# Linear attention and a Fourier feed-forward on one core: the channel transform on twice folded rows, some steps on POOL, and new ranks for the first part

## The chip, the cores and the metric

The kernel runs on one NeuronCore of a Trainium2 chip. Its engines work side by side and are joined by semaphores: TensorE (PE in the profile, with its weight loads as PEld), VectorE (DVE), ScalarE (ACT), GpSimd (POOL) and SyncE (SP, which here only issues DMA transfers). The metric is the device time of one execution in microseconds (us). Several executions are timed, and their median counts.

## The reference

```python
kv  = einsum('bhsd,bhse->bhde', k, v)            # 8 batches, 8 heads, 576 tokens, 64 per head
out = einsum('bhsd,bhde->bhse', q, kv)
x   = out / sqrt(mean(out*out, -1) + 1e-6) * g_norm   # then heads side by side: [8, 576, 512]
X     = fft(fft(x, axis=1), axis=2)              # over the tokens, then over the channels
u     = x + real(X)
un    = (u - mean(u)) / sqrt(var(u) + 1e-6)
y     = u + maximum(un @ w_ch1, 0) @ w_ch2       # 512 -> 2048 -> 512
```

The weights of the feed-forward arrive as 64-bit floats, which the kernel takes apart in 32-bit words.

## The kernel before, in words

**First part: attention and transform, by batch.** For each of the eight batches `plan_kv` (L527) multiplies keys and values (bank `ps_k`, L574), `plan_q` (L631) turns the queries (`ps_q`, L643), and `plan_out` (L657) multiplies them with the result (`ps_o`, L669). Tokens lie in three tiles t of 96 or 97 rows; a row holds token p and its mirror S − p side by side, which is the fold over the tokens. `plan_y` and `plan_fold` (L716, L752) scale the rows by their root mean square and fold them over the channels: channel d plus channel 512 − d, 256 columns per side (L785 on VectorE), then sum and difference of the two sides on POOL (L792). ACT and POOL split the result into a high part `xh` and a low part `xl` for fp32r matmuls (L798, L801). Everywhere a product of two split operands takes three matmuls, `passes`: high·high, high·low, low·high.

**The two transforms.** `plan_seq` (L807) multiplies the folded rows with the token matrix `cs` (290 columns), once for each of two parts (cosine, sine) and two channel halves ch of 128; ACT and VectorE split the product (`ps_f`, L816) into the pair `pt` (L830, L834). `plan_chn` (L840) multiplies `pt` with the channel matrix `cd` (258 columns) for each tile and part: two halves times three passes, summed in one bank (L851). ACT copies the cosine part out (L863), VectorE adds the sine part with either sign (L871), and the sums are added to x (L883, L886: on VectorE for batch 0, else on POOL). `plan_turn` (L917) then transposes x into `unT` (`ps_t`, L942; split at L951, L954), blocks of 512 tokens.

**Weights and feed-forward.** `plan_w` (L964) loads a pair of weights as 64-bit words and makes 32-bit floats of them: absolute value on ACT (`w_clear`, L352), then five VectorE steps (`w_steps`: a clamp L359, shifts and masks L360 to L366, a product L369), a sum, and a split. Three pairs (NA = 3) are made early, in the first part; four more at its end; the others in the second part. With the early ones `plan_early` (L1021) runs the first three of the 16 hidden slices for all nine token blocks inside the first part: `ffn1` (`ps_h`, L424) and `ffn2` (`acc`, L442). The second part runs the remaining slices.

**What sets the order.** The first part is a list of operations with an engine, a cost in ns, a rank, predecessors and buffers. `Plan.run` (L155) is a list scheduler: on each engine, the ready operation of the lowest rank whose buffers are free goes next. `rank(b, stage)` is 10 b + stage, with the stages KV, QT, OUT, SCL, FOLD, SEQ, CHN, NRM as 0 to 7, less 40 for batch 0; the early feed-forward has 1000 and more. `SHIFT` (L58) adds to the ranks of single stages on single engines, keyed by stage, engine and rounded rank. `W_CONV` and `W_RANK` (L42) are the ranks of the early weights' work and loads. The order is pinned up to 95 us of the plan's time; behind that the compiler orders by itself. `plan_spare` (L486) puts in 45 operations of two 512-column matmuls each, whose result nobody reads (`ps_s`, L494), wherever TensorE would wait. Buffers come from rings of fixed sizes (`RINGS`, L72), among them eight PSUM banks (`p8`).

## Time and profile before

| what | before |
|---|---|
| median of 3 runs | 1024.85 us (1022.36 to 1027.26) |
| the profiled execution | 1022.79 us |
| its span, first to last instruction | 1021.0 us |
| busy: PE / PEld | 1002.3 / 844.0 us |
| busy: DVE / ACT / POOL | 475.3 / 324.8 / 314.4 us |
| granted TensorE clock | 1.00 |
| moved by DMA | 140.74 MB, 137 GB/s over the span |

The span is cut into stretches and each engine's busy time is given for them; the groups collect instructions by line and shape, with the mean duration of one. The chain of waits follows the work that ended last back to its start. Matmuls are pipelined, so the duration of one (390 ns for 512 columns) is longer than the distance to the next; the chain's pieces, divided by their count, give that distance. The transforms end at 319 us; the early feed-forward goes on after them.

### The profile page before, as it was taken

What the parts mean: (1) busy time and instruction counts of PE and PEld (TensorE: products, weight loads), DVE (VectorE), ACT (ScalarE), POOL (GpSimd) and SP (SyncE); (2) the same over time, 40 slices, a digit from 0 to 9 for tenths busy, and PEclk for the clock granted to TensorE, in tenths of its full rate; (3) what the DMA queues carried; (4) which work ended last, traced back from release to release, by engine and by line L of the source; (5) the groups of instructions that cost most, each with busy time, mean ns of one, the idle gap of its engine ahead of it and who ended that gap; (6) DMA issues with size and microseconds to landing.
All of it is one profiled execution on the core that took longest, in us unless ns stands there. A gap on an engine that the chain in (4) does not pass through costs nothing.

```text
span 1021.0 us, 15425 instructions
## 1 busy us (share of the span) xinstructions
PE 1002.3 (98%) x6070; PEld 844.0 (83%) x6070; DVE 475.3 (47%) x847; ACT 324.8 (32%) x657; POOL 314.4 (31%) x328
## 2 busy tenths in 40 slices
PE   5999999999999999999999999999999999999997
PEld 5898888889888888888888888888888888888886
DVE  4897656654788879997131313131221311311211
ACT  2666556554644434344221202121121120210110
POOL 0526768775675132235722303020020010100000
PEclk9999999999999999999999999999999999999999
DMA  9989778664346775645553514230320400400101
GB/s 250 212 230 282 181 209 258 162 170 131 137 163 213 268 253 191 236 129 170 161 179 86 180 59 150 82 125 0 141 67 1 165 21 1 165 0 1 42 1 42
DMA packets 109260, 140.74 MB, mean 138 GB/s; under 512 B 51854, under 2 KB 76482, under 8 KB 104580
## 3 DMA queue, kind: packets, MB, share of 16 engines
q1 hardware_dynamic: 105652, 132.28, 41.9%
q0 software_dynamic: 1920, 6.29, 1.9%
q10 hardware_dynamic: 1616, 1.18, 0.5%
q8 instruction: 48, 0.79, 0.3%
q14 instruction: 24, 0.20, 0.1%
HBM read 88.33 MB, written 51.40 MB: 137 GB/s over the span
## 4 chain that ended last, share of the span: by engine, by line
PE 97%; DMA 1%; ACT 0%; POOL 0%; DVE 0%; issue 0%; SPq 0%; DVEq 0%; POOLq 0%
PE ps_h L424 38%; PE acc L442 38%; PE ps_o L669 4%; PE ps_f L816 4%; PE ps_f L851 4%; PE ps_k L574 3%; PE ps_s L494 2%; PE ps_q L643 2%; PE ps_t L942 2%; DMA qt<-in_q_dram 1%; PE ps_w L383 1%; DMA vm<-in_v_dram 0%; POOL x L883 0%; ACT x L686 0%; DVE uu L1324 0%
## 5 line engine op out<-in xcount | busy, mean ns | idle before, releaser
L424 PE MATMUL ps_h<-unTh,w 128*128 128x512 f32 x1152 | 356.6, 391 | 1.2 <-ACT fq L647 1.2
L442 PE MATMUL acc<-w,hh 128*128 128x512 f32 x1152 | 345.5, 390 | 0.0
L437 DVE SCALAR_TENSOR_TENSOR hl<-ps_h,hh 128x512 fp32r<-128x512 f32 x144 | 99.1, 688 | 371.8 <-ACT hh L434 367.5
L442 PEld LDWEIGHTS acc<-w,hh 128*128 128x128 f32 x1152 | 215.1, 188 | 44.3
L424 PEld LDWEIGHTS ps_h<-unTh,w 128*128 128x128 f32 x1152 | 214.8, 188 | 44.8 <-ACT fq L647 1.4
L434 ACT ACTIVATE hh<-ps_h 128x512 fp32r<-128x512 f32 x144 | 85.8, 596 | 454.0 <-PE ps_h L424 439.2
L424 PE MATMUL ps_h<-unTl,w 128*128 128x512 f32 x576 | 224.3, 389 | 0.0
L442 PE MATMUL acc<-w,hl 128*128 128x512 f32 x576 | 213.5, 389 | 0.0
L424 PEld LDWEIGHTS ps_h<-unTl,w 128*128 128x128 f32 x576 | 108.1, 188 | 22.6
L442 PEld LDWEIGHTS acc<-w,hl 128*128 128x128 f32 x576 | 108.1, 188 | 22.6
L1271 POOL DMA_INDIRECT uu<-u_scr,rowidx x24 | 23.2, 968 | 285.1 <-DVE uu L1324 177.9
L709 POOL TENSOR_TENSOR x<-x,gb 96x512 f32<-96x512 f32 (+1 forms) x42 | 55.0, 1330 | 45.7 <-ACT x L686 40.3
L1290 POOL TENSOR_TENSOR uu<-uu,up 128x512 f32<-128x512 f32 x36 | 45.7, 1298 | 45.2 <-ACT up L1287 45.2
L1234 POOL TENSOR_TENSOR w<-wap,w 128x512 fp32r<-128x512 f32 x18 | 26.4, 1467 | 75.3 <-ACT w L1233 69.1
L669 PEld LDWEIGHTS ps_o<-kvt,fq 64*96 64x96 f32 (+1 forms) x864 | 40.9, 162 | 5.7 <-issue 4.0
L1324 DVE SCALAR_TENSOR_TENSOR uu<-acc,rs_yb,uu 128x512 f32<-128x512 f32 x36 | 25.2, 744 | 42.5 <-PE acc L442 42.5
L669 PE MATMUL ps_o<-kvt,fq 64*96 64x64 f32 (+1 forms) x864 | 44.4, 248 | 0.0
L696 DVE TENSOR_REDUCE ss<-ps_o 96x8 f32<-96x512 f32 (+1 forms) x48 | 32.0, 682 | 26.5 <-ACT ps_o L691 26.3
L792 POOL TENSOR_TENSOR xe<-ab 96x256 f32<-96x256 f32 (+1 forms) x46 | 38.0, 845 | 18.7 <-DVE ab L785 17.9
L816 PE MATMUL ps_f<-cs,xh 96*128 96x290 f32 (+1 forms) x192 | 39.0, 300 | 0.0
L1278 DVE BATCH_NORM_STATS2 bst<-uu 128x6 f32<-128x512 f32 x36 | 24.5, 687 | 29.0 <-DMA uu<-u_scr,rowidx 19.8
L851 PE MATMUL ps_f<-cd,pt 128*96 128x258 f32 (+1 forms) x288 | 37.8, 285 | 0.0
(114 smaller groups left out, 1022.4 us busy)
## 6 DMA issues: line engine op xcount, KB each, us to landing
raw<-in_moe_w_ch_dram SPq DMA_DIRECT2D x32, 512.0 KB
unT_scr<-unTh SPq DMA_DIRECT2D x9, 1024.0 KB
unT_scr<-unTl SPq DMA_DIRECT2D x9, 1024.0 KB
part_scr<-part SPq DMA_DIRECT2D x36, 256.0 KB
unTh<-unT_scr SPq DMA_DIRECT2D x9, 1024.0 KB
unTl<-unT_scr SPq DMA_DIRECT2D x9, 1024.0 KB
up<-part_scr SPq DMA_DIRECT2D x36, 256.0 KB
out_dram<-uu SPq DMA_DIRECT2D x36, 256.0 KB
```

Of the source, the lines that this page charges most:

```text
L424: nc.tensor.matmul(ps, w[c][:, kc * P : (kc + 1) * P], unT[a][:, kc, :], start=(idx == 0), stop=(idx == 3 * KC - 1),)
L434: nc.scalar.activation(hh, ps, AF.Relu)
L437: nc.vector.scalar_tensor_tensor(hl, ps, 0.0, hh.bitcast(F32), ALU.max, ALU.subtract)
L442: nc.tensor.matmul(acc, hpair[a][:, i * P : (i + 1) * P], w[c], start=(first and n == 0), stop=(last and n == 2),)
L574: nc.tensor.matmul(ps.t[s * D : (s + 1) * D, pr * D : (pr + 1) * D], km[:, s, j, :] if j < 4 else kr[:, h, :], vm[:, s, j, :] if j < 4 els ...
L669: nc.tensor.matmul(pss[s].t[:n, at : at + D], fqs[side].t[half, m, :n], kvt.t[half, m], start=True, stop=True,)
L696: nc.vector.tensor_reduce(ss.t[0][:n, :, t, s::2], pss[s].t[:n].rearrange("p (u m e) -> p u m e", u=2, e=D), AX.X, ALU.add,)
L709: nc.gpsimd.tensor_tensor(v_, v_, gb[:n].unsqueeze(1).to_broadcast([n, H, D]), ALU.mult)
L792: nc.gpsimd.tensor_tensor(o[:, s], a[:, 0], a[:, 1], ALU.subtract if s else ALU.add)
L816: nc.tensor.matmul(ps.t[:, :NS], xs[t].t[a][:n, part, ch * P : (ch + 1) * P], cs[:n, part, c, t, :], start=(idx == 0), stop=(idx == 8),)
L851: nc.tensor.matmul(ps.t[:n, :ND], pt.t[a][:, part, ch, offs[t] : offs[t] + n], cd[:, part, c, ch, :], start=(idx == 0), stop=(idx == 5),)
L1290: nc.gpsimd.tensor_tensor(us[j][i], us[j][i], part, ALU.add)
```

## The change

**The channel transform.** Two matmul operations of a part are made first, one per channel half. ACT copies the second out of PSUM (`far`), VectorE writes its sum with the first into one bank and the difference into the other, and each is split as before. For even output columns only one of these is needed, for odd ones the other. So `plan_chn` multiplies each with 130 columns of one parity (`NE`) instead of both halves with 258. For this the first fold lays the upper channel half out in reverse order, in three operations, and the matrix is loaded with its columns sorted by parity (`plan_dft_d`). Channel 128 is its own partner; channel 256, which stands in its place in the other half, goes into the odd columns alone and into the sum of element zero (`x0`): `paired` is 0 in partition 127 and 1 elsewhere, and that row of the odd cosine columns gets 1 added.

```diff
@@ plan_fold
-            nc.scalar.activation(
-                x0[:n, t, b : b + 1], xv(0)[:, 0:1], AF.Identity, bias=xv(1)[:, 0:1]
-            )
+            nc.vector.tensor_reduce(x0[:n, t, b : b + 1], x.t[:n, :: DH], AX.X, ALU.add)
...
-            nc.vector.tensor_tensor(
-                two_of(ab), xx[:, :, 1 : DH + 1], xx[:, ::-1, DM - 1 : DH - 1 : -1], ALU.add
-            )
+            for at, lo, hi, step in ((0, 1, P + 1, 1), (P, DH - 1, P, -1), (DH - 1, DH, DH + 1, 1)):
+                width = (hi - lo) * step
+                nc.vector.tensor_tensor(
+                    two_of(ab)[:, :, at : at + width],
+                    xx[:, :, lo:hi:step],
+                    xx[:, ::-1, DM - lo : DM - hi : -step],
+                    ALU.add,
+                )
@@ plan_seq, for each part, after both matmul operations
+        def out_():
+            nc.scalar.copy(far.t, pss[1].t[:, :NS])
+        def add():
+            p0, p1 = (ps.t[:, :NS] for ps in pss)
+            if part == 0:
+                nc.vector.scalar_tensor_tensor(p1, far.t, paired, p0, ALU.mult, ALU.add)
+            else:
+                nc.vector.tensor_tensor(p1, p0, far.t, ALU.add)
+        def sub():
+            p0 = pss[0].t[:, :NS]
+            if part == 0:
+                nc.vector.scalar_tensor_tensor(p0, p0, paired, far.t, ALU.mult, ALU.subtract)
+            else:
+                nc.vector.tensor_tensor(p0, p0, far.t, ALU.subtract)
+        f = op("ACT", 410, r - D2, out_, mms[1:], [pss[1], far])
+        e = op("DVE", 450, r - D2, add, [mms[0], f], [far] + pss)
+        o = op("DVE", 450, r - D2, sub, [e], [far, pss[0]])
+        for ps, parity, after in ((pss[1], part, e), (pss[0], 1 - part, o)):
...
@@ plan_chn
-                for ch in range(2):
-                    for a, c in passes:
+                for e in range(2):
+                    for idx, (a, c) in enumerate(passes):
                         nc.tensor.matmul(
-                            ps.t[:n, :ND],
-                            pt.t[a][:, part, ch, offs[t] : offs[t] + n],
-                            cd[:, part, c, ch, :],
+                            ps.t[:n, e * NE : (e + 1) * NE],
+                            pt.t[a][:, part, e, offs[t] : offs[t] + n],
+                            cd[:, part, c, e, :],
                             start=(idx == 0),
-                            stop=(idx == 5),
+                            stop=(idx == 2),
                         )
...
-            mms.append(op("PE", 720, r, mm, dones + [dft["d", part]], [ps, pt]))
+            mms.append(op("PE", 500, r, mm, dones + [dft["d", part]], [ps, pt]))
...
+        def both(a):
+            return a[:n, : 2 * NE].rearrange("p (e k) -> p k e", e=2)[:, : ND // 2]
```

The copy of the cosine part and the two sums with the sine part (L863, L871) read the bank through `both`, so that the columns come out in their order.

**Steps on POOL.** The clamp of the three early weight pairs (six tiles) goes from VectorE and PSUM to POOL and SBUF, and the subtraction that gives the token matrix's low part goes from VectorE to POOL. Later weights are clamped on VectorE as before.

```diff
@@ plan_dft, token matrix only
         c = op(
-            "DVE", 200 + 1.6 * size if key == "s" else 200 + size, r,
-            lambda: nc.vector.tensor_tensor(lo, raw.t[:n, :size], hi.bitcast(F32), ALU.subtract),
+            "POOL", 2300, r,
+            lambda: nc.gpsimd.tensor_tensor(lo, raw.t[:n, :size], hi.bitcast(F32), ALU.subtract),
@@ plan_w
+        high = ps if late_ else pf
+        d = op("ACT", 670, r, lambda: w_clear(raw.t, high.t), [a], [raw, ps, pf, src])
+        if late_:
+            d = op("DVE", 690, r, lambda: w_clamp(nc.vector, ps.t), [d], [ps])
+        else:
+            d = op("POOL", 1000, r, lambda: w_clamp(nc.gpsimd, pf.t), [d], [pf])
```

**The order.** The ten shifts of ranks are replaced by 25. Among them: the first pair's weight loads go from rank −60 to −27.5, behind keys and values (−40), the queries of one tile (−38.5) and both matrices (−37, −35); the other queries of batch 0 go from −39 (with a shift of −1.5 before) to 2.5; the VectorE steps of the second weight pair from 5 to 138.5, the ACT steps of the third from 6 to 118.

```diff
 SHIFT = {
-    ("", "POOL", 20): 18,
-    ("chn", "ACT", -34): 54.5,
-    ("dft", "DVE", -35): 83.5,
-    ("fold", "DVE", -36): -33.5,
-    ("out", "DVE", -58): 31,
-    ("out", "ACT", 2): 157,
-    ("q", "PE", -39): 3,
-    ("q", "PE", 21): -30,
-    ("q", "ACT", 31): -19.5,
-    ("q_load", "DMA", -39): -1.5,
+    ("chn", "DVE", -34): 31,
+    ("chn", "POOL", 16): 76.5,
+    ("chn", "ACT", 26): 113.5,
+    ("chn", "POOL", 26): 29.5,
+    ("chn", "ACT", 36): 60.5,
+    ("chn", "POOL", 36): 104,
+    ("out", "PE", -38): -7.5,
+    ("out", "ACT", -8): 36.5,
+    ("out", "DVE", -8): 40,
+    ("out", "PE", 22): 129,
+    ("out", "ACT", 32): 10.5,
+    ("out", "POOL", 42): 91.5,
+    ("q", "ACT", 41): -31.5,
+    ("q", "PE", 41): 76.5,
+    ("q", "POOL", 41): 42.5,
+    ("q_load", "DMA", -39): 41.5,
+    ("turn", "ACT", 17): 54.5,
+    ("turn", "PE", 17): 10,
+    ("turn", "ACT", 27): 87.5,
+    ("turn", "PE", 27): 193.5,
+    ("w", "DMA", -60): 32.5,
+    ("w", "DVE", 5): 133.5,
+    ("w", "ACT", 6): 112,
+    ("y", "DVE", -37): 100,
+    ("y", "POOL", 23): -28,
 }
```

More of the change, by code (lines that the diff above doesn't have):

```diff
@@ L73 @@
     "p8": 8, "part": 2, "unT": 2, "h": 2 * NA, "qt": 2, "fq": 4, "kvt": 2, "kv": 6, "kr": 2,
-    "x": 8, "raw": 2, "e2": 4, "wk": 2, "xhl": 3, "pt": 1, "two": 2,
+    "x": 8, "raw": 2, "e2": 4, "wk": 2, "xhl": 3, "pt": 1, "two": 2, "far": 1,
 }
@@ L460 @@
     cs = cst.tile([TR + 1, 2, 2, 3, NS], F32R, name="cs")
-    cd = cst.tile([P, 2, 2, 2, ND], F32R, name="cd")
+    cd = cst.tile([P, 2, 2, 2, NE], F32R, name="cd")
+    paired = cst.tile([P, 1], F32, name="paired")
+    nc.vector.tensor_scalar(paired, ident[:, P - 1 : P], -1.0, 1.0, ALU.mult, ALU.add)
     x0 = cst.tile([TR + 1, 3, B], F32, name="x0")
@@ L503, in plan_dft @@
     def plan_dft(part, dst, src, n, r, key):
+        if key == "d":
+            plan_dft_d(part, r)
+            return
         size = src.shape[-2] * src.shape[-1]
@@ L793, in even @@
             return go
-        f = op("DVE", 690, r, fold, ms, [x, ab, xe], port=True)
-        z = op("ACT", 300, r, zero, ms + [i_x0], [x])
+        f = op("DVE", 860, r, fold, ms, [x, ab, xe], port=True)
+        z = op("DVE", 80, r, zero, ms + [i_x0], [x])
         e = [op("POOL", 830, r, even(s), [f], [ab, xe]) for s in range(2)]
@@ L1108 @@
         pt = Buf("pt", lambda: [one.tile([P, 2, 2, NS], F32R, name=f"pt{i}") for i in range(2)])
-        pts = [plan_seq(b, grp, xhl, pt, lows) for grp in range(4)]
+        pts = sum((plan_seq(b, part, xhl, pt, lows) for part in range(2)), [])
         for t in range(3):
@@ L1217, in sum_w @@
         w_clear(raw, ps)
-        for step in w_steps(raw, ps, pf):
+        w_clamp(nc.vector, ps)
+        for step in w_steps(raw, ps, pf, ps):
             step()
```

113 lines of the change are left out of this document (72 added, 41 removed).

## The prediction

> **What bounds the kernel now.** I read the head of the page first, then the chain of waits piece by piece, then the groups by shape, then the windows of the first 400 us. Columns of the page's first lines: busy time, share, instructions; then the span in 40 slices.
>
> ```profile
> span 1021.0 us, 15425 instructions
> PE 1002.3 (98%) x6070; PEld 844.0 (83%) x6070; DVE 475.3 (47%) x847; ACT 324.8 (32%) x657; POOL 314.4 (31%) x328
> ...
> PE   5999999999999999999999999999999999999997
> ...
> DVE  4897656654788879997131313131221311311211
> ```
>
> TensorE works through the whole span, so a change is worth what it takes from TensorE's stream plus what it does to TensorE's idle time. A busy TensorE can still be slowed inside a group of matmuls, so I need the pace of each kind. The chain of waits gives it (start, length, what):
>
> ```profile
> 1.77 8.50 DMA qt<-in_q_dram
> ...
> 10.36 0.88 PE ps_q L643 x4
> ...
> 24.18 5.61 PE ps_o L669 x128
> ...
> 37.85 0.88 PE ps_k L574 x20
> ...
> 77.36 5.48 PE ps_h L424 x24
> ...
> 276.90 4.84 PE ps_f L816 x36
> 285.53 4.30 PE ps_f L851 x36
> ...
> 360.44 2.73 PE ps_h L424 x12
> ```
>
> A sequence-transform matmul (290 columns) takes 4.84 / 36 = 134.4 ns, a channel-transform matmul (258) 4.30 / 36 = 119.4, a feed-forward matmul (512) 2.73 / 12 = 227.5. From 258 to 512 columns that is 108.1 / 254 = 0.426 ns a column, and that line gives 133.0 at 290, close to the row: these three kinds are limited by streaming their columns, and the loading of their weights is hidden.
>
> Idle time of TensorE is 1021.0 − 1002.3 = 18.7 us: 10.4 before the first matmul, 5.4 in the last 21 us, and some 3 in gaps. The gaps are this small because something fills them. Below: the first and the last stretch (PE, PEld, DVE, ACT, POOL, granted clock, DMA share, GB/s), and all matmuls of the filler, first and last.
>
> ```profile
> 0.00:25.00 25.00, 14.64 (x150) 12.33 (x152) 10.95 (x20) 6.05 (x11) 0.96 (x9) 1.00 1.06 250
> 1000.00:1021.00 21.00, 15.64 (x70) 12.61 (x68) 4.79 (x7) 1.20 (x2) 0.00 (x0) 0.99 0.13 51
> ```
> ```profile
> L494 PE MATMUL ps_s<-still x90: 387/397/588, 13.4 to 90.4; 128*128 128x512 f32 x90
> ```
>
> The filler (ps_s) does no useful work, is issued a fixed number of times and is spent at 90 us; from 77 us the early feed-forward (ps_h) takes over. Both kernels pay for the filler, 90 × 227.5 ns = 20.5 us.
>
> **The channel transform.** It removes 288 matmuls of 258 columns and puts in 288 of 130: two parities × three passes × two parts × 24 tiles, where there were two channel halves × three × two × 24. Before, that is 288 × 119.4 = 34.4 us of the chain. No fp32r matmul so narrow is in the trace. Streaming alone, by the line above, would be 119.4 − 128 × 0.426 = 64.9 ns. But each matmul also loads 96 or 97 columns of weights, and that sets a floor of its own. Weight loads by shape (the number of columns is the last of the loaded shape; then busy, mean ns):
>
> ```profile
> L851 PEld LDWEIGHTS ps_f<-cd,pt 128*96 128x96 f32 x192 | 23.6, 162 | 0.3
> L816 PEld LDWEIGHTS ps_f<-cs,xh 96*128 96x128 f32 x128 | 20.5, 189 | 0.0
> L1131 PEld LDWEIGHTS ps_o<-cs,x0h 96*8 96x8 f32 x4 | 0.4, 89 | 0.2
> ```
>
> From 96 to 128 columns a load grows by 27 / 32 = 0.84 ns a column, from 8 to 96 by 73 / 88 = 0.83. So 97 columns need 81 ns of loading, whatever is streamed meanwhile. The attention output shows this floor at work: ps_o above are 64 pairs on the two halves of the array's rows, 97 weight columns and only 64 streamed ones each, and a pair takes 5.61 / 64 = 87.7 ns. I take 87.7, the nearest row (the same number of weight columns with a shorter stream): 288 × (119.4 − 87.7) = **9.1 us less**. Ends: 64.9 ns gives 15.7 us less; no gain at 119.4; losses are among the rivals.
>
> The Trainium skill ("TensorE: Matmul & The Clock Gate", Part 3, The mechanism) says that a weight load overlaps matmuls in flight only when the row group differs. By that, narrow matmuls would be a poor exchange, since loading and streaming would stand one behind the other; the 258-column row speaks against it, as 81 ns of loading and 258 × 0.426 = 110 of streaming fit in 119.4. The isolated gap on that page of the Trainium skill (Back-to-back issue gap) would make it 130 / 2.4 + 2.5 = 56.7 ns, an estimate that gives 18.1 us less; it gives 110.0 at 258, where the row has 119.4.
>
> **What the second fold adds.** Rows of the first 320 us, by shape, and one of line L785 over the whole span (shortest/median/longest):
>
> ```profile
> L785 DVE TENSOR_TENSOR ab<-x 96x512 f32<-96x512 f32 x15 | 16.0, 1064 | 3.6 <-POOL x L886 3.4
> L774 DVE TENSOR_TENSOR x<-x,ps_y 96x512 f32<-96x512 f32 x32 | 20.0, 676 | 0.1
> L834 DVE TENSOR_TENSOR pt<-ps_f,pt 128x290 fp32r<-128x290 f32 x32 | 13.8, 454 | 9.4 <-ACT pt L830 9.2
> L359 DVE TENSOR_SCALAR ps_a<-ps_a 128x512 f32<-128x512 f32 x9 | 6.2, 694 | 5.4 <-ACT ps_a L352 5.4
> L520 DVE TENSOR_TENSOR cs<-draw,cs 97x870 fp32r<-97x870 f32 x2 | 2.0, 1022 | 0.0
> L954 DVE TENSOR_TENSOR unTl<-ps_t,unTh 128x4 fp32r<-128x4 f32 x7 | 1.2, 164 | 0.0
> L594 DVE TENSOR_TENSOR kvt<-ps_k,gb 128x256 f32<-128x256 f32 x1 | 0.4, 424 | 3.2 <-PE ps_k L574 3.2
> ```
> ```profile
> L785 DVE TENSOR_TENSOR ab<-x x23: 673/717/1861, 32.5 to 299.5; 96x512 f32<-96x512 f32 x15, 97x512 f32<-97x512 f32 x8
> ```
> ```profile
> L830 ACT ACTIVATE pt<-ps_f 128x290 fp32r<-128x290 f32 x32 | 12.9, 415 | 15.0 <-PE ps_f L816 14.7
> L779 ACT ACTIVATE x<-x 96x1 f32<-96x1 f32 x16 | 4.7, 291 | 3.9 <-DVE x L774 3.8
> ```
>
> Per batch and part ACT gets a copy out of PSUM (415 ns) and VectorE an addition and a subtraction of 290 columns (454 each): over 16 parts ACT 6.6 us, VectorE 14.5. The first fold becomes two operations of half the width and one of two elements: 2 × 424 + 164 = 1012 against 1064 at the mean here, but 0.3 us more where the old one ran undisturbed (median 717), so 0 to 8 us over 24. The sum of element zero goes from ACT (24 × 0.291 = 7.0 us less) to VectorE (24 × 0.164 = 3.9 at most). From VectorE go six clamps (4.2 us) and two subtractions on the token matrix (2.0). Net: VectorE +12 to +20 us, ACT about even. The strided reads of the channel results I cost at nothing: the old fold reads an operand backwards and takes 673 at its shortest, the scaling in plain order 676. Where does the VectorE time lie?
>
> ```profile
> 25.00:100.00 75.00, 75.00 (x901) 64.31 (x898) 61.47 (x105) 45.98 (x100) 33.31 (x46) 1.00 0.94 240
> 100.00:325.00 225.00, 222.01 (x1956) 194.99 (x1955) 146.26 (x271) 124.13 (x290) 156.69 (x168) 1.00 0.61 181
> ```
>
> Columns are PE, PEld, DVE, ACT, POOL. From 100 to 325 us VectorE has 79 us free. From 25 to 100 it is 82% busy, but most of the 6.2 us leaves that stretch, and the new ranks push VectorE's steps on the second pair of weights far back. So I cost it at 0. What hides it is the early feed-forward on TensorE; the price without that cover is the longer way from a sequence product to its channel product: a copy, two VectorE operations and a second split, 0.415 + 2 × 0.454 = 1.3 us a batch, 10.4 us over eight.
>
> **What moves to POOL.** Six clamps and two subtractions of 870 columns:
>
> ```profile
> L709 POOL TENSOR_TENSOR x<-x,gb 96x512 f32<-96x512 f32 x28 | 37.3, 1349 | 24.6 <-ACT x L686 19.2 <-DMA qt<-in_q_dram 5.4
> L731 POOL TENSOR_SCALAR m<-ss 97x48 f32<-97x48 f32 x7 | 1.6, 230 | 0.6
> ```
>
> At 1.35 us per 512 columns that is 6 × 1.35 + 2 × 2.3 = 12.7 us; a clamp costs between 0.23 and 1.35, and I take the latter, which has its width. In 25 to 100 us POOL is busy 33 of 75, so it fits. Each weight's chain grows by 0.65, and folds queued behind on POOL wait up to 1.35 each; TensorE has filler then. Cost 0, at worst 6 × 0.65 + 2 × 1.3 = 6.5 us.
>
> **The order of the first part.** SP's queue now begins with two weight loads:
>
> ```profile
> 0.74 0.99 SPq L349 DMA_DIRECT2D raw<-in_moe_w_ch_dram  x2
> ```
>
> This 1 MB goes behind the keys, the queries of one tile and both matrices; the queries of the other two tiles go behind it. At 250 GB/s (first stretch) 1 MB is 4.2 us, by which keys and values arrive earlier. TensorE starts on them, before 10.36, but a pair of heads (0.88 us of matmul) needs 512 KB, 2.1 us of transfer, so it starts and waits. Against that, the moved queries have 2304 + 480 + 660 + 516 + 1024 KB ahead of them and 960 of their own, 6.1 MB or 24.3 us: just where the first ps_o stood (24.18), so the first tile moves up and the others stay or slip by the landing. I count 2 us less idle time, between 4.2 less and 2 more. The remaining new ranks reorder VectorE, ACT, POOL and TensorE work of batches 1 to 4; I put them at 0, between the 3 us of gaps and the loss of the fourth rival.
>
> **Sum.** The profiled execution took 1022.79 us, its span 1021.0. Of the former: −9.1 − 2.0 = 1011.7. The median of the runs shown, 1024.85, is 2.06 above that execution, so as a median I predict **1013.7 us**, 1.1% faster.
>
> **Rivals**, as medians. (1) Streaming alone limits: 64.9 ns, 15.7 + 2.0 less, 1007.2. For it: loads are hidden in all three fp32r rows. Against: the 87.7 of ps_o. 0.10. (2) The longer way to the channel product is not covered: +10.4, 1024.1, no change. For it: the ps_f buffers are held longer, and there are eight banks; against: the early feed-forward lies between, in all but the first batches. 0.11. (3) Slower: a narrow fp32r matmul runs at the pace of plain fp32.
>
> ```profile
> 48.73 0.93 PE ps_w L383 x8
> ```
>
> The only full products of 128 columns in the trace are these, plain fp32, two records to a product, 0.93 / 4 = 232 ns. At 130 columns that is 236 ns, 288 × (236 − 119.4) = 33.6 us more: 1024.85 − 2.0 + 33.6 = 1056.5. It decides from 119.4 ns. All fp32r rows are of 258 columns or wider, so no row excludes it; all of them lie on one line, so none hints at it. 0.06. (4) The early feed-forward starts late: the second and third pairs of weights now wait behind VectorE and ACT work of all batches, the filler is spent, and TensorE idles for the block it had at 75 to 125 us, 72 × 227.5 ns = 16.4 us: 1030.1, at the edge between the same and slower. For it: ranks of 118 and more for these steps; against: a low rank only yields, and VectorE has gaps. 0.10. (5) Loading and streaming stand one behind the other: 87.7 + 64.9 = 152.6 ns, 9.6 us more, 1032.5; the 258-column row speaks against it. It is the overlap rule of the Trainium skill cited above. 0.03.
>
> **How the numbers follow.** Forecast 0.60. Taking 0.5% (5.1 us, about what a measurement of this kernel can tell) as the bound: faster 0.60 + 0.10 = 0.70; same 0.11 + 0.06 of the fourth = 0.17; slower 0.04 + 0.06 + 0.03 = 0.13. The range takes in rival 1 with the 3 us of gaps (1004) and reaches past rival 2 to 1026; left out are rivals 3 and 5, most of 4, and a little below.
>
> **What would show it.** Right: 36 channel matmuls in 3.0 to 3.2 us of the chain; feed-forward unchanged at 227 ns; a first matmul of keys before 10 us; filler still 90 records; TensorE's busy time near 992 us. Wrong: channel matmuls at 65 or above 119 ns; idle time of TensorE that ends on VectorE's split, on the added copy, or on a weight; the first ps_h well behind 77 us with gaps ahead of it.

## The result, and the profile after

The kernel after the change takes 1029.98 us (median of 11 runs, 1028.74 to 1031.65), the kernel before 1023.94 (11 runs, 1022.28 to 1029.65): a ratio of 1.0053, 95% interval 1.0036 to 1.0069. It is 0.5% slower, where 1.1% faster was predicted. The profiled execution took 1031.65 us, with a span of 1029.8, which is 8.8 more than before.

The head of the page after the change, in the columns of the one before, and the chain's shares by engine (before, TensorE had 97% and VectorE 0%):

```profile
span 1029.8 us, 15530 instructions
...
PE 1006.0 (98%) x6070; PEld 844.6 (82%) x6070; DVE 503.0 (49%) x945; ACT 323.1 (31%) x649; POOL 323.5 (31%) x338
...
PE 89%; DVE 5%; issue 2%; DMA 1%; POOL 1%; ACT 1%; DVEq 0%; POOLq 0%
```

From the chain of waits, piece by piece (start, length, what):

```profile
115.17 3.89 DVE ab L838 x4
...
129.13 4.90 PE ps_f L935 x30
134.03 7.43 PE ps_f L875 x36
...
230.23 3.22 PE ps_f L935 x36
...
246.45 4.86 PE ps_f L875 x36
```

The channel matmuls (L935) do what was forecast: 3.22 / 36 = 89.4 ns instead of 119.4, 288 × 30.0 = 8.6 us less. So 8.8 + 8.6 = 17.4 us came from elsewhere. The chain now runs over VectorE's folds, as at 115 us, where before it hardly left TensorE. TensorE's idle time rose from 18.7 to 1029.8 − 1006.0 = 23.8, that is 5.1 us. Its busy time rose by 3.7, where it was to fall to about 992, though 8.6 us of streaming had gone: so 12.3 us are matmuls that took longer than they should. The chain shows some: at 129 and 134 us the same two kinds take 163 and 206 ns instead of 89 and 135.

Why, is in the windows of that stretch (columns as in the prediction; the third number from the end is the granted clock) and in TensorE's timeline, with the idle time ahead of an instruction and its releaser in brackets:

```profile
120.00:124.00 4.00, 3.34 (x47) 2.60 (x44) 4.00 (x5) 0.44 (x2) 3.84 (x5) 1.00 0.63 186
124.00:128.00 4.00, 2.31 (x13) 1.53 (x11) 3.82 (x8) 2.19 (x7) 2.38 (x3) 1.00 0.67 155
128.00:132.00 4.00, 2.87 (x19) 2.87 (x20) 0.83 (x2) 2.71 (x8) 2.54 (x2) 0.67 0.17 66
132.00:136.00 4.00, 4.00 (x22) 4.00 (x22) 2.54 (x6) 0.37 (x1) 2.25 (x2) 0.50 0.00 0
136.00:140.00 4.00, 4.00 (x20) 4.00 (x19) 0.32 (x1) 0.40 (x1) 4.00 (x5) 0.55 0.55 148
```
```profile
122.63 0.55 PE L695 MATMUL ps_q<-ident,qt 97*128 97x97 f32 x4 [0.62 <-DVE ss L748]
...
126.75 0.73 PE L935 MATMUL ps_f<-cd,pt 128*97 128x130 f32 x6 [1.17 <-DVE pt L916]
129.13 4.90 PE L935 MATMUL ps_f<-cd,pt 128*97 128x130 f32 x30 [1.65 <-ACT pt L913]
```

TensorE waits 0.6, 1.2 and 1.7 us within 7 us. Then the granted clock falls to 0.50. How long, follows from the windows: (0.33 + 0.50 + 0.45) × 4 us / 0.50 = 10.2 us, in which TensorE does the work of half that time. So the waits cost twice, once by their length and once by the 5.1 us that the clock takes afterwards. A second stretch of 6.8 us begins at 303. Together they take 17.1 / 2 = 8.5 us. The profile of before has no such stretch up to 352 us. "Busy 98%" hides it, since a slow matmul counts as busy.

The start has it too. TensorE's first instructions after the change, and before it:

```profile
8.22 1.12 PE L626 MATMUL ps_k<-vm,km 128*64 128x64 f32 x16 [8.22 <-DMA km<-in_k_dram]
10.39 0.48 PE L626 MATMUL ps_k<-vr,kr 64*64 64x64 f32 x4 [1.05 <-DMA kr<-in_k_dram]
12.31 1.12 PE L626 MATMUL ps_k<-vm,km 128*64 128x64 f32 x16 [1.44 <-DMA km<-in_k_dram]
...
17.57 1.12 PE L626 MATMUL ps_k<-vm,km 128*64 128x64 f32 x16
...
23.17 3.10 PE L721 MATMUL ps_o<-kvt,fq 64*96 64x64 f32 x64
```
```profile
19.48 0.69 PE L574 MATMUL ps_k<-vm,km 128*64 128x64 f32 x16
```

Sixteen key products take 1.12 us at 8 us and still at 17.6, where the same sixteen take 0.69 at 19.5 before the change. The first matmul comes 2.1 us earlier, as forecast, but TensorE runs slowly until about 23 us. (The clock column says 1.00 here, but the trace's record of the clock has its first entry, at full speed, only at 23.6 us, and in the kernel before at 13.6.) The same holds in every profile of this document: in the ten with the new first loads that entry lies at 17.6 to 24.0 us, in the ten with the old ones at 13.4 to 16.2. By an estimate, against a fixed pace for each kind of matmul, the distances between starts in the first 25 us are too long by 8.5 us after and by 2.1 before: 6.4 more, of which 2.7 are the waits at 10, 12 and 14 us (1.05, 1.44 and 0.25) and 3.7 the slow pace. With the 8.5 of the two later stretches that makes 12.2 of the 12.3 us of lengthened matmuls. By place, then, the 17.4 us are 4.3 at the start (6.4 less the 2.1 of the earlier first matmul), 8.5 in the half-clock stretches and some 4.5 of further waiting behind the start.

The other surprise is the fold. By shape, the groups of its VectorE operations after the change, and the scaling beside it, whose second operand lies in PSUM:

```profile
L838 DVE TENSOR_TENSOR ab<-x 96x254 f32<-96x254 f32 x15 | 15.3, 1019 | 0.0
L838 DVE TENSOR_TENSOR ab<-x 96x2 f32<-96x2 f32 x15 | 12.9, 857 | 0.0
L838 DVE TENSOR_TENSOR ab<-x 96x256 f32<-96x256 f32 x15 | 12.4, 827 | 0.2
...
L826 DVE TENSOR_TENSOR x<-x,ps_y 96x512 f32<-96x512 f32 (+1 forms) x48 | 29.6, 678 | 0.3
```
```profile
L838 DVE TENSOR_TENSOR ab<-x x69: 146/422/3160, 48.6 to 301.6; 96x256 f32<-96x256 f32 x15, 96x254 f32<-96x254 f32 x15, 96x2 f32<-96x2 f32 x15, 97x256 f32<-97x256 f32 x8
```

An operation on two elements takes 146 ns at its shortest and 857 on average. All 72 take 55.8 us, where the 24 of before took 23.6: 32 us more, against the 0 to 8 of the prediction. Both operands of these operations lie in SBUF; the scaling beside them, with one in PSUM, takes its 678 ns as before. The Trainium skill ("SBUF — State Buffer", Who interferes with whom) says that a VectorE instruction with two SBUF inputs contends with a GpSimd instruction that reads SBUF, and that the second to come waits for the first to end. The trace agrees. Of the 69 operations that carry the names `ab<-x`, 33 take over 0.2 us more than the shortest of their width, 32 us more in all, and each of these 33 began while a POOL operation was running; of the other 36, 7 did. Cut in three, an operation can be caught three times. At their shortest (406, 408 and 146 ns) the three take 0.29 us more than the one before (673), 6.6 us over 23 tiles; the rest is waiting. Six of the operations, the POOL work beside them, and what follows on VectorE:

```profile
113.97 8.01 DVE L838 TENSOR_TENSOR ab<-x 97x256 f32<-97x256 f32 x6
121.90 1.27 DVE L748 TENSOR_REDUCE ss<-ps_o 97x8 f32<-97x512 f32 x2
...
117.87 1.62 POOL L848 TENSOR_TENSOR xe<-ab 97x256 f32<-97x256 f32 x2
119.45 2.50 POOL L761 TENSOR_TENSOR x<-x,gb 97x512 f32<-97x512 f32 x2
```

The last of the six, on two elements, starts at 118.8 and takes the longest, 3160 ns: it lasts through the rest of a short POOL operation and two of 1.3 us. Behind it come the reductions `ss`, and on one of them ends TensorE's wait of 0.62 us at 122.6.

The remaining steps of the prediction's last part: the filler has its 90 records, the first `ps_h` comes at 91.2 us instead of 77.2 with no gap ahead of it, and the feed-forward runs at 227 ns.

### The profile page after: what moved, and what is told of

Same layout as the page of the kernel before. It is cut to its first block, busy times and chain, and to the rows that moved or that the text cites. A ratio compares the mean times of both kernels' runs of the same rounds, so it can differ in the third digit from the quotient of the medians.

```text
span 1029.8 us, 15530 instructions
## 1 busy us (share of the span) xinstructions
PE 1006.0 (98%) x6070; PEld 844.6 (82%) x6070; DVE 503.0 (49%) x945; ACT 323.1 (31%) x649; POOL 323.5 (31%) x338
## 4 chain that ended last, share of the span: by engine, by line
PE 89%; DVE 5%; issue 2%; DMA 1%; POOL 1%; ACT 1%; DVEq 0%; POOLq 0%
PE ps_h L442 37%; PE acc L460 36%; PE ps_o L721 3%; PE ps_f L875 3%; PE ps_f L935 2%; PE ps_k L626 2%; DVE ab L838 2%; PE ps_s L515 2%; PE ps_t L1036 1%; PE ps_q L695 1%; DVE x L826 1%; DMA km<-in_k_dram 1%; PE ps_w L401 1%; DMA vm<-in_v_dram 1%; POOL x L977 0%
## 5 line engine op out<-in xcount | busy, mean ns | idle before, releaser
L838 DVE TENSOR_TENSOR ab<-x 96x254 f32<-96x254 f32 (+5 forms) x69 | 51.1, 795 | 0.2
L1335 POOL TENSOR_TENSOR w<-wap,w 128x512 fp32r<-128x512 f32 x18 | 23.3, 1295 | 70.2 <-ACT w L1334 70.2
L875 PE MATMUL ps_f<-cs,xh 96*128 96x290 f32 (+1 forms) x192 | 41.1, 313 | 0.0
L848 POOL TENSOR_TENSOR xe<-ab 96x256 f32<-96x256 f32 (+1 forms) x46 | 34.9, 779 | 17.3 <-DVE x L831 10.8
```

The costliest lines, as they stand in the source:

```text
L838: nc.vector.tensor_tensor(two_of(ab)[:, :, at : at + width], xx[:, :, lo:hi:step], xx[:, ::-1, DM - lo : DM - hi : -step], ALU.add,)
L848: nc.gpsimd.tensor_tensor(o[:, s], a[:, 0], a[:, 1], ALU.subtract if s else ALU.add)
L875: nc.tensor.matmul(ps.t[:, :NS], xs[t].t[a][:n, part, ch * P : (ch + 1) * P], cs[:n, part, c, t, :], start=(idx == 0), stop=(idx == 8),)
```

## The experiments

Ratios are to the kernel before on the same chip, with 95% intervals. Clocks are the mean granted clock of a run; 0.001 of it is 1.03 us. It leaves out the slow start, for which the traces have no clock record.

### One part alone, in the kernel before

**Narrow matmuls.** The loops of the kernel before, with 130 columns per half:

```diff
-                            ps.t[:n, :ND],
+                            ps.t[:n, ch * 130 : (ch + 1) * 130],
-                            cd[:, part, c, ch, :],
+                            cd[:, part, c, ch, :130],
```

> The kernel of before with the channel matmuls on 130 columns instead of 258 (the two halves' products stand side by side instead of being summed, so the result isn't the reference's); ranks, costs of the plan, fold and everything else as before. If TensorE's work is what the time hangs on, as the prediction's first term has it: 1024 - 8.7 = about 1015 us. If TensorE then only waits longer for the other engines in the first part: the time stays at 1021 to 1024 and its gaps grow by what the matmuls lose.

Measured: 1026.15 us against 1024.69, 1.001 (0.9984 to 1.0037). The second of the expected outcomes is the nearer, though the median lies above both. The 8.6 us of matmul are saved, and nothing comes of it. In the profiled execution, 1023.28 us, TensorE waits 8.1 us behind the start instead of 3.0, and half-clock stretches of 3.4 and 6.8 us lose another 5.1. TensorE comes to the same places earlier and waits there. Its timeline:

```profile
158.38 0.55 PE L940 MATMUL ps_t<-ident,x 96*128 96x96 f32 x4 [1.01 <-POOL x L881]
...
164.88 1.58 PE L643 MATMUL ps_q<-ident,qt 96*128 96x96 f32 x8 [2.08 <-DVE unTl L952]
...
167.16 0.63 PE L442 MATMUL acc<-w,hl 128*128 128x512 f32 x1
...
171.48 0.39 PE L442 MATMUL acc<-w,hl 128*128 128x512 f32 x1
```

Behind waits of 1.0 and 2.1 us a matmul that takes 0.39 takes 0.63, and the window from 164 to 168 has a clock of 0.50. The runs of this one kernel lie between 1020.9 us (clock 0.996) and 1031.4 (0.985): 11 thousandths, or 11.3 us by the clock, and 10.5 measured. Its best run is 3.8 us below the median of before, its worst 6.7 above.

**Three operations for the fold.** The loop of the change's diff in `plan_fold` alone, with a planned cost of 690 ns:

> The kernel of before with the fold in three operations (the upper channels in descending order, so that the unchanged channel transform gives another result than the reference's); the plan's cost of the fold stays 690. If the waits behind POOL are the loss: the fold rises from 24 to about 50 us in all and the time by 5 to 13 us, 1029 to 1037. If they fall where TensorE has other work: 1024 to 1026.

Measured: 1033.83 against 1024.69, 1.0076 (1.0047 to 1.0104). Its fold, and the longest of TensorE's waits behind the start:

```profile
L787 DVE TENSOR_TENSOR ab<-x x69: 142/440/3666, 33.5 to 313.4; 96x256 f32<-96x256 f32 x15, 96x254 f32<-96x254 f32 x15, 96x2 f32<-96x2 f32 x15, 97x256 f32<-97x256 f32 x8
```
```profile
PE ps_o L669 <- DVE ss L696: 3.3, 1, 3.3
```

The fold takes 51.2 us instead of 23.6, and TensorE waits for a VectorE reduction. In this profile half-clock stretches begin at 132 and 166 us, in the kernel before at neither.

**The longer way to the channel product.** Copies of existing steps, with nothing new computed:

```diff
+            for _ in range(1 + ch):
-            lambda: nc.scalar.activation(pt.t[0][:, part, ch, :], ps.t[:, :NS], AF.Copy), [a], [ps, pt],
+                nc.scalar.activation(pt.t[0][:, part, ch, :], ps.t[:, :NS], AF.Copy)
...
         def low():
+            for _ in range(2):
```

> The kernel before, with nothing of the change but the length of the way from a sequence product to its channel product: each low part is formed twice on VectorE and every second high part twice on ACT, with the same result and the scheduled costs and the order unchanged. That is 0.415 + 2 x 0.454 = 1.32 us more per batch and part, 16 times, the price that rival 2 of the prediction names, without the narrow matmuls, the three-part fold and the new ranks. Theory A (waits of TensorE cost more than their length, since the granted clock falls to 0.50 after them): TensorE waits 5 to 10 us more in all, stretches of half clock appear in the profile between 100 and 320 us, the mean clock is below 0.995, and the median rises by 6 to 14 us, to 1030 to 1038, more than the waits that the trace shows. Theory B (a wait costs its own length, and the longer way is mostly covered): 0 to 5 us more, 1024 to 1029, clock as before. Theory C (the way is on TensorE's path in every batch, no clock effect): 10.4 us more, 1034, at a clock of 0.998.

Measured: 1039.43 against 1024.86, 1.0128 (1.0086 to 1.0169), at clocks of 0.987 to 0.993. Theory B falls (0 to 5 us), and so does C as a mechanism: it named TensorE's wait in every batch at a clock of 0.998. Theory A is right in kind and 1.4 us past its upper end in size. (The 10.4 us of rival 2 count the way once a batch; this edit, as the change itself, lengthens it in both parts, 16 × 1.32 = 21.1 us of work.) TensorE's waits in the profile, and the windows around the longest:

```profile
PE ps_q L643 <- DMA qt<-in_q_dram: 9.6, 1, 9.6
PE ps_t L944 <- POOL x L885: 5.1, 3, 3.5
PE ps_w L383 <- POOL wp L379: 2.9, 1, 2.9
```
```profile
124.00:128.00 4.00, 1.15 (x5) 1.09 (x6) 1.75 (x4) 0.42 (x2) 4.00 (x4) 0.76 1.05 233
128.00:132.00 4.00, 4.00 (x15) 2.74 (x13) 1.25 (x1) 1.43 (x3) 4.00 (x6) 0.50 1.09 310
132.00:136.00 4.00, 4.00 (x68) 3.71 (x67) 1.44 (x3) 2.71 (x7) 4.00 (x5) 0.89 0.20 71
```

None of its waits is for the split that was made longer. Half of the waiting behind the start is for the additions to x on POOL, which come after the channel product; that the longer split delays them is how I read it, and not shown. The waits behind the first add up to 10.4 us, against 2.6 in the kernel before; the span grew by 17.5. Half-clock stretches of 6.8, 6.8, 6.8 and 3.4 us begin at 126, 167, 228 and 344. Here the planner was not told of the longer way; in the change it is.

**Less work on POOL.** The gain g_norm on 64 of 512 columns only, which takes 41 us from POOL's first 400; in the kernel before, with the narrow matmuls, and after the change:

```diff
-                    v_, v_, gb[:n].unsqueeze(1).to_broadcast([n, H, D]), ALU.mult
+                    v_[:, :1], v_[:, :1], gb[:n].unsqueeze(1).to_broadcast([n, 1, D]), ALU.mult
```

> The kernel of before with the gain on 64 of 512 columns (seven heads of eight stay without it), nothing else. If TensorE's work is the bound there, with gaps of some 3 us behind the start: 1018 to 1023 us, and the narrow matmuls on top of it are worth 8 to 9 us. If POOL is as much a bound as TensorE: below 1015 us.

> The kernel of before with the narrow channel matmuls, and the 42 multiplications by the gain on POOL on 64 of their 512 columns (seven heads of eight stay without their gain, so the result isn't the reference's); ranks and costs of the plan as before. If POOL's chain is what gave the 8.7 us back: POOL loses some 45 us, TensorE's gaps from 100 to 200 us close, and the time falls to 1008 to 1014 us. If TensorE's written order or VectorE is: 1020 to 1026 as in the narrow matmuls alone.

> The changed kernel with the gain on 64 of 512 columns (seven heads of eight stay without it). If the fold waits for POOL's instructions: it falls from 52 to some 40 us in all, and the time by as much as TensorE's gaps hang on it, to 1012 to 1020 us. If the start and the longer way to the channel product are the loss: 1026 to 1030.

Measured: 0.9996 (0.998 to 1.0011), 0.9987 (0.9963 to 1.0011) and 1.003 (1.0007 to 1.0054). POOL's load is no bound of the kernel before. After the change the fold falls from 55.8 to 44.7 us with it, though its instructions are the same, and the median by 2.5, well short of the 10 us or more that were expected if the fold's waits were the loss. By itself the shorter fold would prove little, since in other profiles with the same three operations it takes 46 to 56 us; that POOL's instructions lengthen it, the trace of the kernel after shows above.

### One part undone, in the kernel after

**The fold in one operation**, as before:

```diff
-            for at, lo, hi, step in ((0, 1, P + 1, 1), (P, DH - 1, P, -1), (DH - 1, DH, DH + 1, 1)):
...
+            nc.vector.tensor_tensor(
+                two_of(ab), xx[:, :, 1 : DH + 1], xx[:, ::-1, DM - 1 : DH - 1 : -1], ALU.add
+            )
```

> The changed kernel with the old fold in one operation: the upper half of the channels stays in ascending order, so the channel transform pairs the wrong channels; everything else does the same work. If the waits of three VectorE operations behind POOL lose the time: the fold falls from 52 to about 25 us in all, TensorE's gaps from 100 to 325 us close, and the time falls by up to 13 us, to 1017 to 1021. If the start and the ranks lose it: 1027 to 1030.

Measured: 1021.5 us, 0.997 (0.9947 to 0.9993). This is the largest gain of any single step, 8.5 us below the kernel after, at the edge of the 1017 to 1021 that were expected if the fold's waits are the loss. Its fold takes 27.9 us, and at the place of the first half-clock stretch:

```profile
124.00:128.00 4.00, 2.94 (x32) 2.69 (x30) 1.63 (x5) 3.65 (x10) 4.00 (x5) 1.00 0.88 253
128.00:132.00 4.00, 4.00 (x35) 4.00 (x35) 2.54 (x6) 0.62 (x2) 3.43 (x4) 1.00 0.01 3
```

About 1 us of idle time is left there, and the clock stays at 1.00; of the two half-clock stretches one remains, 6.8 us from 293.

**Two other ways to a shorter fold.** One operation on VectorE and the reversal in POOL's sums (first diff), or the two-element operation on ACT (second):

```diff
-                nc.gpsimd.tensor_tensor(o[:, s], a[:, 0], a[:, 1], ALU.subtract if s else ALU.add)
+                for to, at in (
+                    (slice(0, P), slice(0, P)),
+                    (slice(P, DH - 1), slice(DH - 2, P - 1, -1)),
+                    (slice(DH - 1, DH), slice(DH - 1, DH)),
+                ):
...
```
```diff
-            for at, lo, hi, step in ((0, 1, P + 1, 1), (P, DH - 1, P, -1), (DH - 1, DH, DH + 1, 1)):
+            for at, lo, hi, step in ((0, 1, P + 1, 1), (P, DH - 1, P, -1)):
...
+                nc.scalar.activation(
+                    two_of(ab)[:, s, DH - 1 : DH], xv(s)[:, DH : DH + 1], AF.Identity,
+                    bias=xv(1 - s)[:, DH : DH + 1],
+                )
```

> The changed kernel with the fold on VectorE in one operation, and the reversal moved to the sum and difference of the two sides on POOL, three pieces each; it computes the reference's result. POOL's work grows by some 10 us. If the three VectorE operations are the loss: near the 1021.5 us of the fold in one, 1020 to 1024. If POOL's longer way takes their place: 1026 to 1030.

> The changed kernel with the fold's third operation, of two elements, as two on ACT; it computes the reference's result. If each VectorE operation of the fold waits for an instruction of POOL's own: the fold on VectorE falls from 52 to about 40 us in all and the time by some 3 us, 1025 to 1028. If the number of operations is not what counts: 1029 to 1031.

Measured: 1035.74, 1.0115 (1.0073 to 1.0157), and 1029.69, 1.0052 (1.0035 to 1.0069). With the reversal on POOL VectorE's fold is short (26.0 us), and the time is longer than either expectation had it. POOL's sums and differences take 49.6 us instead of 34.9, but of TensorE's waits only 1.0 us ends on POOL itself, so that POOL is what makes it late is likely and not shown. With two operations VectorE's fold falls to 40.1 us, and the time stays: the half-clock stretch from 129 goes, and another opens at 159.

```profile
160.00:164.00 4.00, 3.74 (x10) 3.02 (x11) 4.00 (x8) 2.06 (x6) 2.87 (x5) 0.58 1.07 231
300.00:304.00 4.00, 3.98 (x21) 2.91 (x21) 3.70 (x7) 1.00 (x2) 2.44 (x3) 0.50 0.00 0
304.00:308.00 4.00, 4.00 (x20) 3.56 (x20) 2.70 (x9) 0.00 (x0) 2.36 (x3) 0.66 0.47 140
```

So the time does not follow the fold's length by itself; it matters where the fold lets TensorE run dry.

**No sum and difference**: without the copy `far` and the two VectorE operations.

```diff
-        f = op("ACT", 410, r - D2, out_, mms[1:], [pss[1], far])
-        e = op("DVE", 450, r - D2, add, [mms[0], f], [far] + pss)
-        o = op("DVE", 450, r - D2, sub, [e], [far, pss[0]])
-        for ps, parity, after in ((pss[1], part, e), (pss[0], 1 - part, o)):
+        for ps, parity, after in ((pss[1], part, mms[1]), (pss[0], 1 - part, mms[0])):
```

> The changed kernel without the copy, the sum and the difference between the two sequence products (each goes to the channel transform as it is, so the result isn't the reference's). It takes 6.6 us from ACT and 15 us from VectorE and shortens the way by 1.3 us a part. If that way is the loss: 1019 to 1023 us. If the fold is: 1027 to 1030.

Measured: 1028.28, 1.0026 (1.0006 to 1.0047): 1.7 us below the kernel after by the medians, 2.8 by the ratios, whose intervals overlap. Here the planner's costs follow the edit, and half-clock stretches stay (10.2 us from 126, 3.4 from 307).

**The additions to x on VectorE for all batches**, a test of whether TensorE's transpositions wait for POOL:

```diff
-        eng = nc.vector if b == 0 else nc.gpsimd
+        eng = nc.vector
```

> The changed kernel with the two additions to x on VectorE in all batches, as batch 0 has them; it computes the reference's result. POOL loses 51 us, VectorE gains 29, and there are fewer POOL instructions for the fold to wait for. If POOL is the bound of the first part: 1015 to 1022 us, perhaps below the kernel of before. If VectorE is: 1030 to 1036.

Measured: 1043.53, 1.0195 (1.017 to 1.022), slower than either expectation, at clocks of 0.977 to 0.981, the lowest of any kernel here but for one run. VectorE becomes late at the end of the transforms:

```profile
PE ps_o L1231 <- DVE x0h L1223: 6.1, 1, 6.1
```

### The order

**The first loads as before** (the ranks of the first weights' loads and of the other queries put back), **the change with the ten old shifts, and the kernel before with the 25 new ones**:

```diff
-    ("q_load", "DMA", -39): 41.5,
+    ("q_load", "DMA", -39): -1.5,
-    ("w", "DMA", -60): 32.5,
```

> The changed kernel with the shifts of two transfers as before: the first pair of weights at the head of SP's queue and the queries of batch 0 ahead of the keys. If the later first loads cost the 4.3 to 5.7 us that TensorE lost in the first 50 us: 1024 to 1026 us, and the gaps behind 100 us stay. If the start is not worth more than its 2 us of earlier first matmul: 1030 to 1032.

> The changed kernel with the ten shifts of ranks of before in place of the 25 new ones; the channel transform, the fold in three operations and the steps on POOL stay. If the new ranks lose the time (idle TensorE at the start and from 100 to 325 us), the gain of the channel matmuls, 288 x (119.4 - 89.4) = 8.6 us, shows: about 1015 us. If the fold in three operations and the longer way to the channel product lose it, whatever the ranks, the time stays at 1025 to 1030, and the fold (ab<-x on VectorE) still takes some 50 us in all.

> The kernel of before with the 25 new shifts of ranks and nothing else. If the ranks lose the time by themselves: 1024 + 8.6 + 6 = about 1038 us, with the later first loads alone some 5 us of it. If the fold and the longer way lose it: the ranks are neutral but for the first 25 us, 1024 to 1029 us.

Measured: 1031.86, 1.0068 (1.0047 to 1.0089); 1034.35, 1.0093 (1.007 to 1.0116); 1035.21, 1.0103 (1.0079 to 1.0127). The first lies in its second range, the other two in neither of theirs. The old loads win 2 to 4 us at the start, by an estimate like the one above, and half-clock stretches of 10.2, 6.8 and 6.8 us from 111, 166 and 302 take them back. Either order with the other's computation is 9 to 10 us slower than the kernel before. With its own order the change loses 6 us, with the old one 9.

### The clock

**Filler in place of the waits.** Useless matmuls on spare columns ahead of the channel products of two batches, where the half-clock stretches of the kernel after begin; and the same with the fold in one operation:

```diff
+FILLER = {(1, 0, 0): 10, (1, 1, 0): 14, (6, 0, 1): 10, (6, 1, 0): 10, (6, 1, 1): 6}
...
+                    for _ in range(FILLER.get((b, part, e), 0) if t == 0 else 0):
+                        nc.tensor.matmul(
+                            ps.t[:, 2 * NE :],
...
```

> The changed kernel with 50 matmuls of 126 twice columns, into unused columns of the bank, ahead of those groups of the channel transform of batches 1 and 6 before which TensorE waited (1.2 to 1.7 and 0.6 to 0.9 us each); it computes the reference's result. If the half clock behind those waits is what costs most: the two stretches at 0.5 (128 to 140 and 302 to 312 us) go, mean clock 0.998, and 8 to 9 us with them, about 1021 us, though work is added. If the waits themselves are the loss: the filler only takes their place, 1029 to 1031.

> The fold in one operation (the channel transform pairs the wrong channels) with the same filler. If the half clock is the cost: the stretch at 292 to 300 us goes and the time falls from 1021.5 by 4 us or more, to 1015 to 1018. If not: 1021 to 1023.

Measured: 1029.98, 1.0056 (1.0037 to 1.0074), and 1025.35, 1.0006 (0.9991 to 1.0021). The first, in its windows:

```profile
124.00:128.00 4.00, 3.55 (x32) 3.55 (x32) 2.39 (x6) 4.00 (x11) 2.01 (x3) 1.00 0.32 62
128.00:132.00 4.00, 4.00 (x43) 4.00 (x42) 2.63 (x6) 0.78 (x3) 3.40 (x3) 1.00 0.18 70
...
160.00:164.00 4.00, 3.54 (x23) 3.13 (x24) 3.84 (x7) 1.36 (x3) 4.00 (x5) 0.50 0.97 214
```

Work put where TensorE waited keeps the clock at 1.00 there, though one wait of 1.9 us is left ahead of it: this supports that the waits bring the half clock, which the count of windows in the last section shows. The mean clock is 0.994 to 0.998, where the runs of the kernel after have 0.989 to 0.993, and some 6 us of added work (50 matmuls, 119 ns apart) cost nothing. But the time stays where the rival expectation had it, and the 8 to 9 us that less half clock was to bring don't come: a new wait of 3.1 us opens at 157 and a stretch of 6.8 us behind it. In the second the clock is 0.997 or 0.998 in all 12 runs, and 3.9 us are lost against the same kernel without filler, outside both expected ranges: to the filler and to a new wait of 3.5 us.

**Narrow in all batches but two, and in these two alone** (kernel before; batches 1 and 2, where the narrow kernel waits first):

```diff
+                if b in (1, 2):
+                    idx = 0
+                    for ch in range(2):
...
+                    return
```

In the second kernel the condition is `b not in (1, 2)`.

> The narrow channel matmuls alone (the halves' products side by side, so not the reference's result), but in batches 1 and 2 the wide ones of before, ahead of the waits at 126 and 157 to 165 us. It has 2.2 us more matmul work than with all narrow. If the half clock gave the gain back: those stretches stay at full clock and the time is 1024.5 - 6 x 1.1 = about 1018 us, less than with all narrow (1026). If TensorE only waits elsewhere: 1024 to 1027.

> The mirror of the last one: the kernel of before with the narrow channel matmuls in batches 1 and 2 alone (there the halves' products stand side by side, so not the reference's result), 2.2 us less matmul work than before. If the half clock behind the gaps that open there is the cause: slower than before in spite of less work, 1026 to 1031 us, with stretches at 0.5 about 128 to 136 and 160 to 172 us. If less work at worst leaves TensorE waiting: 1022 to 1025.

Measured: 1020.34, 0.9982 (0.9958 to 1.0006), and 1025.99, 1.0018 (1.0001 to 1.0035). The first: eight runs of 1019.1 to 1021.6 at 0.998 and more, four of 1026.0 to 1028.3 at 0.991 and 0.992, with nothing between. The second has 2.2 us less to do than the kernel before and is no faster:

```profile
128.00:132.00 4.00, 2.26 (x9) 1.79 (x10) 0.70 (x2) 4.00 (x10) 4.00 (x5) 0.86 0.87 230
132.00:136.00 4.00, 4.00 (x14) 3.19 (x13) 2.44 (x4) 2.66 (x6) 4.00 (x4) 0.71 1.03 422
```

It waits 1.55 us there for queries and 0.44 for ACT's copy of them, and the clock falls for (0.14 + 0.29) × 4 / 0.50 = 3.4 us; the kernel before waits 1.23 once in the same window and keeps it. So the harm sits in these two batches: without them 4.8 of the 6.5 us of matmul come through by the medians, though the interval still reaches no change.

## Why the prediction was wrong, point by point

- **Channel matmuls, −9.1: right.** 89.4 ns against 87.7, −8.6 us. The prices of 64.9, 152.6 and 236 ns (rivals 1, 5 and 3) are out. So is the estimate of 56.7 ns by the Trainium skill's formula for an isolated gap ("TensorE: Matmul & The Clock Gate", Back-to-back issue gap).
- **"TensorE works through the whole span, so a change is worth what it takes from TensorE's stream plus what it does to TensorE's idle time": this step failed.** The saving alone brought nothing. In the first 320 us a shorter stream turns into waits, which end on VectorE, ACT, POOL or a load; and behind waits the clock falls. The sum had no term for that, and it is larger than the idle time itself: 12.3 us of lengthened matmuls against 5.1.
- **The second fold's VectorE work at 0, as "what hides it is the early feed-forward on TensorE": failed,** and its size was wrong too: the first fold was put at 0 to 8 us more and took 32. The 424 and 164 ns of the sum were close to the shortest of the new operations (406 and 146); what it lacked is their waiting behind POOL, though the row of the old fold itself, 673/717/1861, already showed how such an operation is prolonged. Put into the kernel before, the three operations cost 9.1 us of time; taken out of the kernel after, they give 8.5 back.
- **The longer way, rival 2 (0.11): the right place.** 4.6 us of TensorE's waits at L935 end on the split (2.1 on VectorE's half, `pt` L916, and 2.5 on ACT's, `pt` L913), where there were none. The price was taken as the length of the way, 10.4, counted once a batch instead of once a part; put in by itself and unplanned it cost 14.6, and taken out of the change it gave 1.7 to 2.8, with overlapping intervals. The lengths don't measure it.
- **The start, −2 (2 more at the worst): wrong in sign.** It came 2.1 us earlier and lost 6.4 behind that, 4.3 net. I named the waits, not the slow pace.
- **POOL's steps at 0:** the clamp, 1.35 us in the working, takes 1918 ns. That is 3.4 us more over six of them, all on POOL; no experiment tried it by itself.

```profile
L371 POOL TENSOR_SCALAR wp<-wp 128x512 f32<-128x512 f32 x6 | 11.5, 1918 | 23.9 <-ACT wp L368 23.8
```

- **The order at 0:** it has no price of its own. Under the new computation the new order is worth 3 to 4 us, under the old one it costs 10.
- **Rival 4,** TensorE idle ahead of the early feed-forward: this started 14 us later, but from 75 to 100 us the distances between matmuls are too long by 0.9 us, 0.7 before. It didn't happen.

Two things stay open: which of the middling waits make the clock fall (below), and how the 17.4 us divide among the parts of the change; by place they are told above. Put in alone, the fold cost 9, the longer way 15 and the order 10, which is more than all of them together; each opens waits that the others would have opened too, so the single costs don't add.

## What to carry to other kernels

An engine that is busy for 98% of the span doesn't give back one for one what is taken from its work: first time a kernel that shortens that work alone, before building the transformation that pays for it. Price small operations by how often they can be held up by another engine, not by their size alone, and look for that in the spread of the shortest, median and longest of a row that has the same operands. An order written by hand fits one set of durations, so a change and its order are timed together, and a difference of under 1% is read beside the granted clock of each run.

## What the runs showed of the hardware

- **The half clock comes in pieces of 3.4 us.** In all twenty profiles the stretches up to 400 us last one to four times 3.41 us (once seven times), so each piece costs 1.7 us of full work; and within a profile every change of the clock lies a multiple of 3.41 us behind the first. The Trainium skill ("TensorE: Matmul & The Clock Gate", Part 1, What's actually happening) describes a half rate that is decided by free-running windows of 3413 ns; the rows agree, and a window that doesn't start with the kernel would also explain why one and the same kernel keeps its clock in eight runs and loses it in four (1019 to 1022 and 1026 to 1028 us).
- **What counts is TensorE's idle time in one such piece, and little suffices.** Cut into windows of 3.41 us from the clock's first entry up to 400 us, the twenty profiles have 820 windows at full clock. None of the 755 with less than 0.9 us of idle time was followed by half clock, all 15 with over 1.9 us were, and of the 50 between, 19 were: the least was 0.92 us (narrow matmuls alone, at the head of a longer wait) and, with the wait over, 1.01 (the same with less work on POOL), while 1.89 us (the filled kernel) could still pass. In the kernel before no window has more than 1.08 us; in the kernel after the one that ends at 129.4 us has 2.45, from the wait of 1.17 and most of that of 1.65. The same page of the Trainium skill (Why this matters for your kernels) asks for no gaps of more than about 3 us; in these runs a third of that within a window was too much at times. What decides between 0.9 and 1.9 us stays open.
- **A slow start can last.** Of two kernels with the same first matmul and the same waits, the kernel after was still slow at 17.57 us and reached the attention output at 23.17; the one with all additions on VectorE was at full pace at 17.50 and reached it 2.5 us earlier:

```profile
17.50 0.72 PE L626 MATMUL ps_k<-vm,km 128*64 128x64 f32 x16
...
20.68 2.94 PE L721 MATMUL ps_o<-kvt,fq 64*96 64x64 f32 x64
```
